# Layer 1's second mixer product as seven block products for two token tiles

## The chip, the cores and the metric

The kernel runs on one core of a Trainium2 chip. The metric is the device time of one execution in microseconds, the median of several runs. A core has TensorE (PE; its weight loads are shown as PEld), VectorE (DVE), ScalarE (ACT), GpSimd (POOL) and SyncE (SP), which here issues the DMAs. Each engine works through its own instructions in the order in which they are written, and waits where an operand is not there yet.

## The reference

Two layers, each of an attention and a token mixer, with the residual added after both. All is float32. The part that the change touches is the second matrix product of the mixer (`w2`), in the second layer:

```python
h = _layernorm(x, axis=-1)                      # (B, S, D)
u = jnp.einsum("bsd,sf->bdf", h, w1) + b1       # (B, D, F)
u = _gelu(u)
y = jnp.einsum("bdf,fs->bds", u, w2) + b2       # (B, D, S)
return y.transpose(0, 2, 1)                     # (B, S, D)
```

S = 2048 tokens, D = 512 channels, F = 1792. The output of the mixer, transposed, is w2^T u + b2, a matrix of 2048 x 512 with inner size 1792, added to x.

## The kernel before, in words

x is kept in SBUF as 16 token tiles of 128 x 512. Matrix products are done in a reduced float32 form (fp32r). To keep the precision, both operands are split in two: the first half is the value rounded to fp32r (a cast, mostly on ACT), the second half is what the rounding left (a subtraction, on DVE or POOL). A product is then three matmuls: first x first, first x second, second x first.

The order of all work is written out by hand (manual schedule), so the text's order is each engine's order. Layer by layer, `att.run` computes the attention and, between its parts, the first mixer product; `mix.rest` ends both. In `rest`, the last two pairs of token tiles are multiplied: first eight products of six matmuls, then twenty more (L1205), of which every second or so ends a tile f of 128 rows of u. When tile f is complete, `finish` adds it from PSUM on DVE (L1213). The local function `following` is called after each of the twenty products. It splits the w1 weights three products ahead (cast on ACT, L1190; subtraction on POOL, L1192) and loads those seven ahead; then it takes one waiting tile, in two calls of three: `gelu` (ACT: activation L1424, cast L1425), and one call later `gelu_rest` (DVE, L1429). What is left over is done after the last product.

For the second product, `load2` loads w2 in halves of a token tile's weights, 128 partitions x 7 tiles x 128 columns (448 KB), and `split2` splits such a half (ACT L1446, DVE L1447). `second(s)` does one token tile s: for each of the 14 tiles of F three matmuls of 512 columns (L1458) into one PSUM bank, 42 in all, then one DVE instruction adds the bias and x (L1464). In layer 1 the tile is then stored (L1608). The halves are split one and a half token tiles ahead, so a token tile costs ACT two casts and DVE two subtractions and one addition. The first two halves are loaded and split while the first product still runs. In layer 0 the same loop carries the projections of layer 1 between the token tiles; the change leaves layer 0 as it was.

PSUM holds three double banks (tag `sc`) and two single ones (`ac0`, `ac1`). At the end of layer 1 the tiles of the attention (`kst`, `qs`, `vaug`) hold nothing that is still needed, and neither do the mixer's accumulators `uacc` once their gelu is done.

Of the kernel before, what the change touches and what calls it, by code (L numbers as in the profile page):

```python
# [8 lines left out]
F32 = mybir.dt.float32  # L9
# [9 lines left out]
P = 128  # L19
# [12 lines left out]
LAG = 2  # L32
KEPT = 6
GOING = 8

# [16 lines left out]
PLAIN = (2, -2)  # L52
FIRST = (1, 2)
NP = 8
NMORE = 4
# [17 lines left out]
def kernel(  # L73
# [1004 lines left out]
    class Mixer:  # L1078
# [21 lines left out]
        def open(self):  # L1100
            n = self.l
            self.opened = True
            self.ap = pool(f"uacc{n}")
            self.wp = pool(f"w1p{n}")
            self.hp = pool(f"hp{n}")
            self.uacc = [self.ap.tile([P, D], F32, tag=f"ua{f}", name=f"ua{n}_{f}") for f in range(NF)]

# [172 lines left out]
        def rest(self, att):  # L1280
# [99 lines left out]
            def following():  # L1380
# [5 lines left out]
                if ahead is not None:  # L1386
                    begun.append(ahead)

            def rests():
# [26 lines left out]
        def open_u(self):  # L1416
            n = self.l
            self.up = pool(f"up{n}", side="right")
            self.w2p = pool(f"w2p{n}", side="right")
            self.u = [self.up.tile([P, 2, D], F32R, tag=f"u{f}", name=f"u{n}_{f}") for f in range(NF)]  # L1420

        def gelu(self, f):
            tmp = self.uacc[f]
            nc.scalar.activation(tmp, tmp, AF.Gelu_apprx_tanh, bias=b1c[:, f : f + 1])  # L1424
            nc.scalar.copy(self.u[f][:, 0, :], tmp)  # L1425

        def gelu_rest(self, f):
            tmp = self.uacc[f]
            nc.vector.tensor_tensor(self.u[f][:, 1, :], tmp, f32(self.u[f][:, 0, :]), op=ALU.subtract)  # L1429

# [39 lines left out]

        def close(self):
            self.w2p.release()
            self.up.release()
# [111 lines left out]
    for layer in range(2):  # L1585
        mix = Mixer(layer)
        att.run(mix, proj)
        mix.rest(att)
        more = layer == 0
        if more:  # L1590
            warm(AF.Exp)
            proj = Proj(layer + 1)
# [134 lines left out]
```

## Time and profile before

| | us |
|---|---|
| median of 3 runs | 2514.87 (2514.69 to 2514.93) |
| span of the profiled execution | 2509.2 |
| PE busy in it | 2492.8 (99%) |
| DVE, ACT, POOL busy | 1550.9, 2101.7, 148.2 |
| matmuls of line 1458, both layers: count, busy, mean | 1344, 307.4, 0.390 |

The profile is of one execution; its span leaves out some microseconds that the runs' time has. A row of the groups gives the line, the engine, what is written from what, the shapes, how often, the busy time in us and the mean of one in ns, and after a second bar the time for which the engine was idle ahead of these instructions and what ended that wait. Matmuls overlap one another, so their mean duration (0.390) is longer than the distance from one to the next. A row of a timeline gives start, duration, engine, line and operation, and how many instructions were merged.

### The profile page before, as it was taken

How to read it: one execution, taken by the hardware profiler on the slowest of the kernel's cores; microseconds unless marked ns; L12 is line 12 of the kernel's file. 1: busy time of each engine (PE TensorE's matmuls, PEld its weight loads, DVE VectorE, ACT ScalarE, POOL GpSimd, SP SyncE). 2: the span in 40 equal slices, each digit the busy share in tenths (PEclk: the TensorE clock that was granted, in tenths of full speed). 3: DMA queues.
4: the chain of work that ended last, by engine and by line, in shares of the span. 5: the costliest groups of instructions: out<-in, count | busy, mean ns of one | idle time of the engine just before them, and what ended most of it. 6: DMA issues, size and time to landing. Idle time of an engine off the chain costs nothing. (4 is left out here: it accounts for less than half of the span.)

```text
span 2509.2 us, 41946 instructions
## 1 busy us (share of the span) xinstructions
PE 2492.8 (99%) x16158; PEld 1240.5 (49%) x16158; DVE 1550.9 (62%) x2458; ACT 2101.7 (84%) x2344; POOL 148.2 (6%) x235
## 2 busy tenths in 40 slices
PE   8999999999999999999999999999999999999999
PEld 6444344444444444588863443444444444445887
DVE  6566566667766776564445664666677667765522
ACT  6999999999999999653349999999999999995511
POOL 5000000000000000141000000000000000002200
PEclk9999999999999999999999999999999999999999
DMA  3221201111111111144423211111111111102343
GB/s 117 75 66 41 65 28 40 31 42 31 39 31 39 31 40 32 41 112 149 126 61 118 58 48 48 31 39 33 39 31 39 32 43 33 40 26 67 106 125 96
DMA packets 168679, 143.56 MB, mean 57 GB/s; under 512 B 17650, under 2 KB 132368, under 8 KB 167952
## 3 DMA queue, kind: packets, MB, share of 16 engines
q1 hardware_dynamic: 168464, 140.72, 19.0%
q8 instruction: 132, 2.16, 0.4%
q14 instruction: 83, 0.68, 0.1%
HBM read 97.67 MB, written 26.22 MB: 49 GB/s over the span
## 5 line engine op out<-in xcount | busy, mean ns | idle before, releaser
L922 ACT ACTIVATE p<-sc 128x1024 f32<-128x1024 f32 x1444 | 1405.8, 1049 | 62.9 <-PE sc L912 62.2
L920 DVE COPY p<-sc 128x1024 f32<-128x1024 f32 x604 | 739.1, 1224 | 522.3 <-PE sc L912 436.4
L928 PE MATMUL acc<-p,vaug 128*32 128x512 f32 x8192 | 1000.1, 599 | 0.5 <-DVE q L531 0.5
L912 PE MATMUL sc<-qs,kst 51*128 51x512 f32 x4096 | 683.5, 432 | 6.8 <-SPq L630 2.7
L922 ACT ACTIVATE p<-p 128x1024 f32<-128x1024 f32 x604 | 655.9, 1086 | 14.1 <-DVE p L920 9.2
L912 PEld LDWEIGHTS sc<-qs,kst 51*128 51x128 f32 x4096 | 338.3, 184 | 559.5 <-ACT p L922 387.3
L928 PEld LDWEIGHTS acc<-p,vaug 128*32 128x32 f32 x8192 | 219.0, 109 | 489.3 <-issue 472.9
L1458 PE MATMUL py<-u,w 128*128 128x512 f32 x1344 | 307.4, 390 | 0.0
L1458 PEld LDWEIGHTS py<-u,w 128*128 128x128 f32 x1344 | 251.9, 188 | 52.3
L1446 ACT CAST w<-w2r 128x896 fp32r<-128x896 f32 x64 | 60.3, 945 | 184.6 <-PE py L1458 177.3
L1205 PE MATMUL pu<-hb,w 128*128 128x512 f32 x792 | 209.6, 406 | 0.0
L1205 PEld LDWEIGHTS pu<-hb,w 128*128 128x128 f32 x792 | 140.9, 188 | 57.7 <-issue 31.9
L1192 POOL TENSOR_TENSOR w<-w1r,w 128x256 fp32r<-128x256 f32 x86 | 70.0, 822 | 1581.5 <-ACT w L1190 1581.1
L1447 DVE TENSOR_TENSOR w<-w2r,w 128x896 fp32r<-128x896 f32 x64 | 72.0, 1124 | 111.4 <-ACT w L1446 111.2
L848 DVE RECIPROCAL o<-o 128x128 f32<-128x128 f32 x120 | 113.3, 944 | 9.4 <-DMA o<-ev 9.4
L889 PE MATMUL po<-wo,hl 128*128 128x512 f32 x360 | 100.4, 412 | 0.1
L830 DVE COPY ev<-acc 128x512 f32<-128x512 f32 x64 | 43.7, 682 | 62.1 <-PE acc L928 62.1
L418 PE MATMUL pq<-hT,wq 128*128 128x512 f32 x312 | 81.1, 404 | 0.0
L889 PEld LDWEIGHTS po<-wo,hl 128*128 128x128 f32 x360 | 62.6, 188 | 33.9 <-issue 16.0
L1205 PE MATMUL pu_l<-hb,w 128*128 128x512 f32 x336 | 77.1, 389 | 0.0
L1464 DVE SCALAR_TENSOR_TENSOR x<-py,b2c,x 128x512 f32<-128x512 f32 x32 | 24.0, 750 | 81.2 <-PE py L1458 81.2
L1190 ACT CAST w<-w1r 128x256 fp32r<-128x256 f32 x86 | 34.5, 406 | 47.1 <-PE pu_l L1205 14.3
(191 smaller groups left out, 1179.0 us busy)
## 6 DMA issues: line engine op xcount, KB each, us to landing
w1r<-in_B_w_dram SPq DMA_DIRECT2D x224, 128.0 KB
w2r<-in_B_w_dram SPq DMA_DIRECT2D x64, 448.0 KB
qs<-qd SPq DMA_DIRECT2D x384, 64.0 KB
qd<-q SPq DMA_DIRECT2D x64, 256.0 KB
o<-ev SPq DMA_DIRECT2D x128, 128.0 KB
x<-in_A_x_dram SPq DMA_DIRECT2D x16, 256.0 KB
hd<-hT SPq DMA_DIRECT2D x2, 2048.0 KB
out_dram<-x SPq DMA_DIRECT2D x16, 256.0 KB
```

Source lines behind the costliest of these rows:

```text
L418: yield nc.tensor.matmul(out, a, c, start=(k == 0), stop=(k == len(terms) - 1))
L848: nc.vector.reciprocal(o[:, 1, c], o[:, 1, c])
L889: nc.tensor.matmul(po, a, c, start=(k == 0), stop=(k == 3 * len(parts) - 1))
L912: nc.tensor.matmul(sc[:, j, :], kst[kt // 4][rows, kt % 4 * P : (kt % 4 + 1) * P], qs[i % NQ][rows, j0 // 2, :], start=True, stop=True,)
L920: nc.vector.tensor_copy(pt, sc)
L922: nc.scalar.activation(pt, sc, AF.Exp, scale=0.25)
L928: nc.tensor.matmul(self.acc[i][c : c + 32, :], vaug[:, kt].rearrange("p d k -> p (d k)"), pt[:, j, :], start=(kt == 0), stop=(kt == NKT - ...
L1192: eng.tensor_tensor(w[:, 1], raw, f32(w[:, 0]), op=ALU.subtract)
L1205: nc.tensor.matmul(pu, a, c, start=(start and k == 0), stop=(stop and k == 5))
L1446: nc.scalar.copy(w[:, 0], raw)
L1447: nc.vector.tensor_tensor(w[:, 1], raw, f32(w[:, 0]), op=ALU.subtract)
L1458: nc.tensor.matmul(py, a, d, start=(c == 0 and f == 0 and k == 0), stop=(c == 1 and f == NFH - 1 and k == 2),)
```

## The change: what it does

In layer 1 the second product is done for two token tiles at once by the Strassen-Winograd scheme. The weights of a pair of token tiles are four blocks A11, A12, A21, A22: the first digit is the token tile, the second says whether they belong to even or odd tiles of F. Each block is 128 x 7 x 128. u is cut likewise: B11 and B12 are the left and right 256 columns of the even tiles of F, B21 and B22 those of the odd ones. Instead of eight block products there are seven:

- outer sums of the weights, for each pair of token tiles: S1 = A21 + A22, S2 = S1 - A11, S3 = A11 - A21, S4 = A12 - S2. They are written over blocks no longer needed and are done by POOL (for the first pair of token tiles by DVE), 128 x 896 each;
- inner sums of u, once: T1 = B12 - B11, T2 = B22 - T1, T3 = B22 - B12, T4 = B21 - T2 (`inner_sums`, seven steps for each of the seven pairs k of tiles of F). The first difference of a pair k is on POOL for k < 4, else on DVE; the other two are on DVE. T1 takes the place of B12 in `u`; T2 and T3 are put in the freed accumulator of the pair, T4 in `kst` and `qs`; working tiles lie in the mixer's pool, or in `vaug` and a tile of the w2 pool. Each T is split into two halves (four casts on ACT, four subtractions on DVE, of 256 columns). `following` takes two of these steps a call; of those left, all but seven are done in `begin_pairs`, the last seven beside the first product;
- the gelu's cast and `gelu_rest` of even tiles are done for 256 columns, since B12 is not used itself.

`pairs` runs eight pairs of token tiles, each of seven products. A product is, for each of seven k, one matmul of 512 columns (the weights' first half times both halves of the 256 columns, side by side) and one of 256 columns (the weights' second half times the first half). One DVE instruction adds each half of the bank to x, so each use of a product is two instructions of 256 columns. In the first pair of token tiles the products go to six banks, in the other seven to three that are used again (X four times, where the second use goes on from the first without clearing it). The weights of product n + 3 are split when product n is written; blocks of the pair after next are loaded in the fifth product of a pair, four loads of 448 KB. `load_pair(0)` stands where the first two halves were loaded; the first split stands after the last gelu, and no weights are split within the first product any more. A token tile is stored after the sixth, its neighbour after the seventh product.

```diff
+PAIR = (
+    ("A11", "B11", "X", True, ("11b",)), ("A12", "B21", "Z", True, ("11",)),
+    ("S2", "T2", "X", False, ("12b",)), ("S1", "T1", "Y", True, ("22b",)),
+    ("S3", "T3", "X", False, ("22",)), ("S4", "B22", "Y", False, ("12",)),
+    ("A22", "T4", "X", False, ("21b",)),
+)
+FIRST_PAIR = (
+    ("A11", "B11", "X", True, ("11b",)), ("A12", "B21", "Z", True, ("11",)),
+    ("S1", "T1", "Y", True, ("12b", "22b")), ("S3", "T3", "W", True, ("21b", "22")),
+    ("S2", "T2", "X", False, ("12", "21", "22")), ("S4", "B22", "V", True, ("12",)),
+    ("A22", "T4", "U", True, ("21",)),
+)
...
             self.open_u()
             warm(AF.Gelu_apprx_tanh)
-            self.load2(0)
-            self.load2(1)
+            if n:
+                self.load_pair(0)
+            else:
+                self.load2(0)
+                self.load2(1)
             for k, pu in enumerate(going):
                 self.product(pu, start=False, stop=False)
                 self.following()
-                if k in (5, 7):
+                if not n and k in (5, 7):
                     self.split2((k - 5) // 2)
...
                 if ahead is not None:
                     begun.append(ahead)
+                for _ in range(2):
+                    if self.inner_steps:
+                        self.inner_steps.pop(0)()
...
             for g in late:
                 self.gelu(g)
                 self.gelu_rest(g)
+            if n:
+                self.begin_pairs()
+                return
             self.split2(2)
...
+            def first():
+                a = got["a"] = pair("ta")
+                eng = nc.gpsimd if k < 4 else nc.vector
+                eng.tensor_tensor(a, halves[:, :, 1], halves[:, 0], op=ALU.subtract)
+
+            def first_split():
+                t1 = self.u[2 * k][:, :, HD:]
+                split(t1, got["a"][:, 0])
+
+            def second():
+                b = got["b"] = pair("tb")
+                nc.vector.tensor_tensor(b[:, 0], halves[:, 1, 1], got["a"][:, 0], op=ALU.subtract)
+                nc.vector.tensor_tensor(b[:, 1], halves[:, 1, 0], b[:, 0], op=ALU.subtract)
+                self.t23[k] = self.ap.tile([P, 2, 2, HD], F32R, tag=f"ua{k}", name=f"t{n}_{k}")
+                split(self.t23[k][:, 1], got["a"][:, 1])
+                split(self.t23[k][:, 0], b[:, 0])
+                split(self.t4[k], b[:, 1])
...
+            return [first, first_split, second, first_low, third_low, second_low, fourth_low]
...
+        def split_pair(self, n):
+            q, j = divmod(n, len(PAIR))
+            if 2 * q >= NKT:
+                return
+            src = self.raw[q, (PAIR if q else FIRST_PAIR)[j][0]]
+            p, bufs = (self.w2q, 3) if n % 4 else (self.w2p, 1)
+            w = self.w2[n] = p.tile([P, 2, NFH, P], F32R, tag="w2", bufs=bufs, name=f"w2_{n}")
+            nc.scalar.copy(w[:, 0], src)
+            nc.vector.tensor_tensor(w[:, 1], src, f32(w[:, 0]), op=ALU.subtract)
+
+        def begin_pairs(self):
+            self.split_pair(0)
+            for name in ("S1", "S3"):
+                self.outer_sum(0, name, nc.vector)
+            while len(self.inner_steps) > 7:
+                self.inner_steps.pop(0)()
+            self.hp.release()
+            self.wp.release()
+            self.w2q = pool("w2q")
+            self.load_pair(1)
+            self.split_pair(1)
+            self.split_pair(2)
...
+            for j, (left, right, key, start, outs) in enumerate(PAIR if q else FIRST_PAIR):
+                n, py = len(PAIR) * q + j, banks[key]
+                self.split_pair(n + 3)
+                w = self.w2.pop(n)
+                for k in range(NFH):
+                    t = self.operand(right, k)
+                    nc.tensor.matmul(
+                        py.rearrange("p (k c) -> p k c", k=2), w[:, 0, k], t,
+                        start=start and k == 0, stop=False, skip_group_check=True,
+                    )
+                    nc.tensor.matmul(
+                        py[:, :HD], w[:, 1, k], t[:, 0], start=False, stop=(k == NFH - 1),
+                        skip_group_check=True,
+                    )
+                if q == 0:
+                    self.beside_first(j)
+                elif j == 2:
+                    self.outer_sum(q + 1, "S1")
+                    self.outer_sum(q + 1, "S3")
+                if j == 4:
+                    self.load_pair(q + 2)
+                    self.outer_sum(q + 1, "S2")
+                if j == 5:
+                    self.outer_sum(q + 1, "S4")
+                for out in outs:
+                    s, c = 2 * q + int(out[0]) - 1, slice((int(out[1]) - 1) * HD, int(out[1]) * HD)
+                    if out[2:]:
+                        nc.vector.scalar_tensor_tensor(
+                            x[s][:, c], py[:, :HD], b2c[:, s : s + 1], x[s][:, c], op0=ALU.add, op1=ALU.add
+                        )
+                    else:
+                        nc.vector.tensor_tensor(x[s][:, c], x[s][:, c], py[:, :HD], op=ALU.add)
+                    nc.vector.tensor_tensor(x[s][:, c], x[s][:, c], py[:, HD:], op=ALU.add)
+                if j > 4:
+                    s = 2 * q + j - 5
+                    nc.sync.dma_start(xout[:, s, :], x[s])
+
+        def beside_first(self, j):
+            if j == 0:
+                self.outer_sum(0, "S2", nc.vector)
+                for step in self.inner_steps:
+                    step()
+                self.outer_sum(0, "S4", nc.vector)
+            if j == 2:
+                self.outer_sum(1, "S1")
+                self.outer_sum(1, "S3")
```

More of the change, by code (lines that the diff above doesn't have):

```diff
@@ new lines, in pair_pool, with load_pair @@
+        def pair_pool(self, q):
+            return self.w2q if q % 2 else self.w2p
+        def load_pair(self, q):
+            if 2 * q >= NKT:
+                return
+            for j, name in enumerate(RAWS):
+                s, c = 2 * q + j // 2, j % 2
+                src = w2_d[:, s * P : (s + 1) * P].rearrange("(t c p) s -> c p t s", p=P, c=2)[c]
+                raw = self.pair_pool(q).tile([P, NFH, P], F32, tag=f"r{name}", name=f"r{name}_{q}")
+                nc.sync.dma_start(raw, src)
+                self.raw[q, name] = raw
@@ L1589 @@
         more = layer == 0
+        if not more:
+            mix.pairs()
+            mix.close()
+            break
         if more:
```

81 lines of the change are left out of this document (76 added, 5 removed).

## The prediction

> **What bounds the kernel now.** I read the page first, then groups by line, then the queues around the end of layer 1's first mixer product, then its steady second product.
>
> ```profile
> span 2509.2 us, 41946 instructions
> PE   8999999999999999999999999999999999999999
> PE 42%; DVE 1%; ACT 0%; issue 0%; DMA 0%; DVEq 0%; ACTq 0%
> PE acc L928 16%; PE sc L912 11%; PE py L1458 6%; PE pu L1205 4%; PE po L889 2%; PE pu_l L1205 2%; PE pq L418 1%; PE pu_m L1205 0%; DVE p L920 0%; ACT p L922 0%; PE pu_b L1205 0%; PE pu_a L1205 0%; PE pu_e L1205 0%; PE po_l L889 0%; DVE stb L1118 0%
> L1458 PE MATMUL py<-u,w 128*128 128x512 f32 x1344 | 307.4, 390 | 0.0
> L1458 PEld LDWEIGHTS py<-u,w 128*128 128x128 f32 x1344 | 251.9, 188 | 52.3
> ```
>
> TensorE is never idle ahead of line 1458 (0.0) and carries the chain. Half of its 1344 matmuls, 672, are layer 1's. The profiled execution spans 2509.2 us and the median of the runs is 2514.87, so 5.7 us lie outside the span; the sum below is a difference, laid on the median. The pace is in DVE's evacuations, one for each token tile:
>
> ```profile
> 2400.54 0.75 DVE L1464 SCALAR_TENSOR_TENSOR x<-py,b2c,x 128x512 f32<-128x512 f32 x1 [2.69 <-PE py L1458]
> 2410.06 0.75 DVE L1464 SCALAR_TENSOR_TENSOR x<-py,b2c,x 128x512 f32<-128x512 f32 x1 [2.69 <-PE py L1458]
> ...
> 2505.25 0.75 DVE L1464 SCALAR_TENSOR_TENSOR x<-py,b2c,x 128x512 f32<-128x512 f32 x1 [8.77 <-PE py L1458]
> ```
>
> 9.52 us for 42 matmuls is 226.7 ns each; 16 token tiles are 152.3 us. Beside it DVE, ACT and POOL are nearly idle. The stage ahead is another matter:
>
> ```profile
> 2333.00:2353.00 20.00, 20.00 (x90) 16.56 (x89) 12.66 (x20) 17.63 (x34) 10.56 (x12) 1.00 0.22 61
> 2330.93 21.92 PE L1205 MATMUL pu_l<-hb,w 128*128 128x512 f32 x96
> 2352.69 9.50 PE L1458 MATMUL py<-u,w 128*128 128x512 f32 x41
> 2353.61 0.72 ACT L1424 ACTIVATE ua<-ua,b1c 128x512 f32<-128x512 f32 x1
> 2354.36 0.62 ACT L1425 CAST u<-ua 128x512 fp32r<-128x512 f32 x1
> 2354.89 0.94 ACT L1446 CAST w<-w2r 128x896 fp32r<-128x896 f32 x1
> ```
>
> The columns of the first are busy time of PE, loads, DVE, ACT, POOL. In the last 20 us of the first product ACT is busy for 17.63 and DVE for 12.66. PE goes straight from one product to the other, while the last gelu ends two microseconds later: it is wanted only at the end of the first token tile, whose weights were split long before.
>
> **The change on TensorE.** For two token tiles there were 84 matmuls of 512 columns; now there are 7 products x 7 tiles, each with one of 512 and one of 256: 49 pairs, 392 over the eight pairs of token tiles. No row has 256 columns. Two rows are near:
>
> ```profile
> 10.30 2.84 PE L137 MATMUL pt<-ident 128*128 128x128 f32 x24
> L137 PEld LDWEIGHTS pt<-ident x24: 192/192/192, 10.2 to 12.8; 128*128 128x128 f32 x24
> L137 PE MATMUL pt<-ident x24: 275/275/275, 10.3 to 12.9; 128*128 128x128 f32 x24
> ```
>
> 24 matmuls, each with its own load recorded at 192 ns, follow one another every (2840 - 275) / 23 = 111.5 ns. So a load that is shown with 188 ns need not hold the array for longer than 111.5. The low end is half of 226.7, 113.4; the high end is a matmul held until its load's recorded end, 188. I take 118, close to the half, since part of the 226.7 may be fixed. A pair is 344.7 ns and the stage 392 x 344.7 = 135.1 us: **17.2 us less** (19.0 by the low end; 10.3 more than before by the high one). A product lasts 2.41 us.
>
> The Trainium skill (TensorE: Matmul & The Clock Gate, Back-to-back issue gap) gives columns / 2.4 + 2.5 ns. By it a pair would be 325 ns and the stage 127 us, 25 us less; at 512 columns it says 215.8 where the row above has 226.7, so the row decides.
>
> **What the other engines get.** The rows for their prices:
>
> ```profile
> L1447 DVE TENSOR_TENSOR w<-w2r,w 128x896 fp32r<-128x896 f32 x64 | 72.0, 1124 | 111.4 <-ACT w L1446 111.2
> L1192 DVE TENSOR_TENSOR w<-w1r,w 128x256 fp32r<-128x256 f32 x138 | 58.7, 425 | 4.8
> L1190 ACT CAST w<-w1r 128x256 fp32r<-128x256 f32 x86 | 34.5, 406 | 47.1 <-PE pu_l L1205 14.3 <-PE pu_b L1205 7.4 <-DMA w1r<-in_B_w_dram 6.8
> L1192 POOL TENSOR_TENSOR w<-w1r,w 128x256 fp32r<-128x256 f32 x86 | 70.0, 822 | 1581.5 <-ACT w L1190 1581.1
> L327 POOL TENSOR_TENSOR wq<-wqr,wq 128x512 fp32r<-128x512 f32 x2 | 2.5, 1284 | 0.0
> 2336.57 1.28 DVE L1213 TENSOR_TENSOR ua<-ua,pu_l 128x512 f32<-128x512 f32 x2 [0.69 <-PE pu_l L1205]
> 2309.89 0.74 POOL L1192 TENSOR_TENSOR w<-w1r,w 128x256 fp32r<-128x256 f32 x1 [0.60 <-ACT w L1190]
> 2309.95 1.23 DVE L1342 TENSOR_TENSOR hb<-ht,hb 128x512 fp32r<-128x512 f32 x1
> ```
>
> Two DVE instructions of 0.69 us end after 1.28, so each overlaps the next by about 0.08: I count 0.345 for 256 columns, 0.61 for 512, 1.02 for 896, and 0.31 for ACT's cast. An evacuation of 256 columns is put at 0.4: 0.75 less 256 x 1.04 ns (the step from 0.69 at 512 to 1.09 at 896), less the overlap. From 256 to 512 POOL goes from 0.74 to 1.28, 2.1 ns a column, so 896 columns cost about 2.15. The last two rows: a DVE subtraction of two SBUF tiles, 0.69 elsewhere, takes 1.23 beside POOL's, that is until 0.55 after POOL's end at 2310.63. It waits its turn; what the two take turns at is called the port below.
>
> I then laid the queues out in the order of the code.
>
> *A, the tail of the first product.* In its last fifteen products of six matmuls (1.36 us each), 30 of the 49 steps of the inner sums are pulled in. ACT gets 17 casts, 5.3 us, less 1.3 for shorter gelu casts: 21.6 us for 20. Worse is the order. Four of the differences are on POOL, 1.28 us each, behind a w1 subtraction of 0.74 that waits for an ACT cast; ACT's cast of the result stands ahead of the next w1 cast. ACT so waits 1.0 to 2.4 us four times, some 6 in all, and DVE's new subtractions and POOL's stop one another. That is 7.6 us over; w1 casts run three products ahead (4.08, less 0.41 for the cast and 0.74 for POOL: 2.9 of lead), so PE stalls about 5. SP adds four w2 loads at once where there were two, then two:
>
> ```profile
> w2r<-in_B_w_dram SPq DMA_DIRECT2D x64, 448.0 KB
> 2315.00:2320.00 5.00, 5.00 (x23) 4.14 (x23) 4.62 (x15) 1.92 (x6) 2.79 (x4) 1.00 0.84 228
> 2321.33 0.78 ACT L1190 CAST w<-w1r 128x256 fp32r<-128x256 f32 x2 [2.00 <-DMA w1r<-in_B_w_dram]
> ```
>
> With two, the next w1 cast already came 1.0 us behind its beat; 0.92 MB more is 3 to 4 us at these rates, against the lead of 2.9: about 1 us on PE. A with DVE and POOL's mutual waits: **6.5** (2 if ACT's waits fill its idle time, 9 if not).
>
> *B, from the last matmul to the first product.* The weights' split now stands behind the last gelu. The floor is on the rows above: addition 0.69, gelu and cast 1.37, split 0.94, subtraction 1.09: 4.1 us, all idle on PE. With ACT's backlog (three casts, two gelus, a wait for DVE, gelu 12) it is 9.3 if all of it is left: I take **8**.
>
> *C, the first pairs.* Before the second product's weights, DVE has two sums of 896 (2.04), twelve steps' worth of inner sums (twelve instructions of 256 columns and one of 512: 4.75) and the subtraction, 1.02: 7.8 us, while PE has 2.41. So at least **5.4** more. Further stalls follow: the last tile's inner sums (2.7) and S2 (1.02) stand in DVE's queue between, and POOL's S1 and S3 for the next pair, 2 x 2.15, want the same port as soon as the loads land; then evacuations of up to six instructions of 0.4 keep DVE behind until the second pair. In the layout the second product waits 6.8 in all (5.4, and ACT's casts between DVE's steps), the third 0.7, or 4.5 if S1 and S3 get in between the last tile's differences, the fifth 1.1 for its bank, the eighth to tenth 2.3, or 4.8 with the port: 10.9 without the port, 17 with it. I take **14**.
>
> *D, steady state.* DVE has 7 x 1.02 + 14 x 0.4 = 12.7 us of a pair's 16.9, ACT 7 x 0.85 = 6, POOL 4 x 2.15 = 8.6. POOL and DVE's subtractions together hold the port for 15.7, and POOL's sums come in pairs, so an evacuation can stand behind a subtraction that stands behind POOL, while PE waits for its bank. Up to 0.9 a pair for six pairs, 5.4; or 0. I take **3.5**. The loads (1.84 MB in 17 us) move what they did before, a pair ahead, and are hidden, as are SP's stores until the last; the last evacuation is two instructions of 0.4 for one of 0.75: 0.1.
>
> The Trainium skill (SBUF — State Buffer, Who interferes with whom) states it as an exclusive lock between GpSimd and DVE instructions with two SBUF inputs, none for those with one. By it C and D are near their upper ends and the sum is 5 us more; without it they are 10.9 and 0, and the sum is 7 us less. The two rows above agree with it.
>
> Sum: -17.2 + 6.5 + 8 + 14 + 3.5 + 0.1 = +14.9 on 2514.87: **2530 us**.
>
> **Rivals.**
>
> *The start is cheap.* If inner sums fit ACT's and DVE's idle time (DVE has 7.3 us idle in those 20, POOL 9.4) only the floors are left: -19.0 + 2 + 4.1 + 5.4 = -7.5, **2507 us**, faster. It decides once A to D stay under 17.2 less 5. Against it: the queues are in order, and each step crosses three engines.
>
> *Loss and gain cancel.* ACT meets POOL's results without waiting (A 2, B 6) and C is 10.9: -17.2 + 18.9 + 0.1 = +1.8, **2517 us**.
>
> *POOL and DVE do not collide.* A 5, B 8.4, C 10.9, D 0: +7, **2522 us**.
>
> *Loads hold the 256-column matmuls*, at 188 ns or as long as 512 columns take, so that the seven products save nothing: the stage is 27.4 us longer than counted, D vanishes: 2530 + 27.4 - 3.5 = **2554 us**. The 111.5 ns row speaks against it.
>
> **How the numbers follow.** Forecast (2524 to 2540) 0.47, start cheap 0.21, cancel 0.13, no collision 0.13, loads 0.06. About 0.2% (5 us) is what a measurement here can tell from no change. Faster is the first rival, 0.21; same the second, 0.13; slower the rest, 0.66. Range 2507 to 2541: the first rival's time to the upper ends of all four, -17.2 + 9 + 9.3 + 17 + 5.4 = +23.5, and a little for a slower 256; outside lie the loads and what beats the floors. The forecast alone spans 2524 to 2540.
>
> **What would show it.** PE's pitch of the new matmuls: 345 ns a pair in an undisturbed product. PE idle ahead of the first product 4 to 9 us, released by ACT or DVE, and ahead of the second at least 5, released by DVE: if either is missing, B or C is wrong. PE waiting for w1 from POOL or ACT after 2335 us shows A. DVE subtractions of 896 columns with means well over 1.1 us, ending a fixed time after POOL's, show the port. A stage under 150 us from the first product's last matmul to the last evacuation (2352.85 to 2506.00, 153.2, before) would make the whole wrong.

## The result, and the profile after

The changed kernel takes 2572.73 us (median of 4, 2571.23 to 2573.88) beside 2514.85 of the kernel before: 1.0234 times as long, 95% interval 1.0219 to 1.0248. It is slower, as forecast, but by 57.9 us instead of 15, and the time lies above the range. One of the twelve executions of the last kernel below (e15) took 4724.9 us; its ratio is of the other eleven.

The page of the changed kernel, its TensorE row in 40 slices, and its chain by engine:

```profile
span 2572.1 us, 42521 instructions
PE   9999999999999999999999999999999999997688
...
DVE 4%; PE 3%; ACT 1%; issue 0%; DMA 0%; POOL 0%; ACTq 0%
```

Before, the chain was TensorE's and its row never fell below 9 after the first slice. Now the last four slices are 7, 6, 8, 8, and VectorE heads the chain. Stretches of the end of layer 1 (busy time of PE, PEld, DVE, ACT, POOL, then the granted clock), first of the changed kernel, then the first product's tail before:

```profile
2318.30:2364.30 46.00, 40.62 (x169) 30.52 (x167) 30.54 (x61) 25.48 (x61) 25.19 (x30) 1.00 0.40 106
2364.00:2372.00 8.00, 0.65 (x3) 0.19 (x1) 5.95 (x13) 6.61 (x13) 0.00 (x0) 0.83 0.61 172
2372.00:2376.90 4.90, 4.32 (x14) 3.24 (x14) 4.55 (x8) 0.82 (x4) 0.00 (x0) 0.59 0.00 0
2376.90:2394.00 17.10, 0.16 (x2) 0.00 (x0) 16.30 (x25) 6.59 (x14) 5.75 (x2) 0.57 0.10 27
2414.00:2438.00 24.00, 19.56 (x101) 16.48 (x100) 18.67 (x22) 6.89 (x8) 11.10 (x6) 0.93 0.38 110
2438.00:2459.00 21.00, 17.34 (x97) 14.70 (x97) 17.19 (x22) 6.25 (x7) 9.62 (x4) 1.00 0.37 107
```

```profile
2314.60:2352.50 37.90, 37.90 (x169) 31.38 (x168) 25.20 (x45) 26.95 (x54) 21.83 (x26) 1.00 0.46 129
```

The same 169 matmuls of the tail take 46.0 us instead of 37.9. Then come 8 us with TensorE idle, one product of 14 matmuls at little over half the granted clock (0.59), and 17 us idle in which VectorE works 16.3. The last two rows of the changed kernel are its second and third pairs of token tiles: TensorE stands idle for 4.4 us of 24 and 3.7 of 21. What TensorE waited for after 2364 us (total, times, longest):

```profile
PE py L1595 <- DVE x L1621: 35.1, 8, 17.1
PE py L1595 <- ACT w L1551: 15.0, 8, 7.6
PE pyw L1595 <- DVE x L1621: 1.9, 1, 1.9
```

And single matmuls of TensorE, then the VectorE instructions ahead of the two waits (start, duration):

```profile
2376.78 0.28 PE L1599 MATMUL py<-u,w 128*128 128x256 f32 x1
2394.19 0.77 PE L1595 MATMUL py<-u,w 128*128 128x512 f32 x1 [17.13 <-DVE x L1621]
...
2427.62 0.40 PE L1595 MATMUL pyy<-u,w 128*128 128x512 f32 x1
2437.46 0.40 PE L1595 MATMUL py<-u,w 128*128 128x512 f32 x1
2439.80 0.28 PE L1599 MATMUL py<-u,w 128*128 128x256 f32 x1
2442.68 0.47 PE L1595 MATMUL py<-u,w 128*128 128x512 f32 x1 [2.60 <-DVE x L1621]
```

```profile
2381.25 1.09 DVE L1552 TENSOR_TENSOR w<-rA,w 128x896 fp32r<-128x896 f32 x1 [0.35 <-ACT w L1551]
2382.26 2.96 DVE L1552 TENSOR_TENSOR w<-rS,w 128x896 fp32r<-128x896 f32 x1
...
2393.11 0.48 DVE L1616 SCALAR_TENSOR_TENSOR x<-py,b2c,x 128x256 f32<-128x256 f32 x1
2393.62 0.42 DVE L1621 TENSOR_TENSOR x<-x,py 128x256 f32<-128x256 f32 x1
...
2439.53 2.15 DVE L1552 TENSOR_TENSOR w<-rS,w 128x896 fp32r<-128x896 f32 x1
2441.61 0.47 DVE L1616 SCALAR_TENSOR_TENSOR x<-py,b2c,x 128x256 f32<-128x256 f32 x1
2442.11 0.42 DVE L1621 TENSOR_TENSOR x<-x,py 128x256 f32<-128x256 f32 x1
...
2445.87 0.42 DVE L1621 TENSOR_TENSOR x<-x,py 128x256 f32<-128x256 f32 x1
```

The second product's weights were ready at 2382.3 (the 1.09 us subtraction). TensorE did not begin until 0.15 us after the first product's evacuation had ended, at 2394.04. The same 0.15 us stands behind the evacuation that ends at 2442.53, in a later pair; there the evacuation is late behind a weight subtraction of 2.15 us. The second product writes Z, not X; Z and X are the two halves of the tile `both`. That is what the first experiment takes apart. From 2427.62 to 2437.46 four products without a wait take 9.84 us, 351 ns for each pair of matmuls.

The second row of the waits is two things: one wait of 7.6 us ahead of the first product, and seven of 1.06 ahead of the third product of a pair. For these the profile names ScalarE's cast, which ended last. The evacuation of Z (2445.87 us in the rows above) ended 0.12 us earlier, at 2446.29, and the product began at 2446.44, again 0.15 us behind the evacuation; in the first experiment these waits are released by evacuations too.

The profile of the kernel before is of an execution that is quicker than its median. In the changed kernel the profiled execution took 2573.88 us and spans 2572.1, so 1.8 us lie outside the span, not the 5.7 of the prediction; by that the one profiled before took about 2511 us. So the two spans differ by 62.9 us and the medians by 57.9.

### The profile page after: what moved, and what is told of

It reads as the page before. It is cut to its first block, busy times and chain, and to the rows that moved or that the text cites. A ratio compares the mean times of both kernels' runs of the same rounds, so it can differ in the third digit from the quotient of the medians.

```text
span 2572.1 us, 42521 instructions
## 1 busy us (share of the span) xinstructions
PE 2497.7 (97%) x16270; PEld 1241.6 (48%) x16270; DVE 1667.4 (65%) x2635; ACT 2132.5 (83%) x2396; POOL 221.5 (9%) x267
## 5 line engine op out<-in xcount | busy, mean ns | idle before, releaser
L1663 PE MATMUL py<-u,w 128*128 128x512 f32 x672 | 154.8, 390 | 0.0
L1663 PEld LDWEIGHTS py<-u,w 128*128 128x128 f32 x672 | 125.7, 188 | 26.1
L1551 ACT CAST w<-rA 128x896 fp32r<-128x896 f32 x48 | 45.2, 941 | 108.2 <-PE py L1599 82.1
L1651 ACT CAST w<-w2r 128x896 fp32r<-128x896 f32 x32 | 30.0, 943 | 76.9 <-PE py L1663 69.3
L1595 PE MATMUL py<-u,w 128*128 128x512 f32 x112 | 48.3, 459 | 42.7 <-DVE x L1621 35.1
L844 DVE COPY ev<-acc 128x512 f32<-128x512 f32 x64 | 43.7, 682 | 62.8 <-PE acc L942 62.8
L1552 DVE TENSOR_TENSOR w<-rA,w 128x896 fp32r<-128x896 f32 x48 | 75.1, 1565 | 2.7 <-ACT w L1551 0.4
```

Of the source, the lines that this page charges most:

```text
L1551: nc.scalar.copy(w[:, 0], src)
L1552: nc.vector.tensor_tensor(w[:, 1], src, f32(w[:, 0]), op=ALU.subtract)
L1595: nc.tensor.matmul(py.rearrange("p (k c) -> p k c", k=2), w[:, 0, k], t, start=start and k == 0, stop=False, skip_group_check=True,)
L1663: nc.tensor.matmul(py, a, d, start=(c == 0 and f == 0 and k == 0), stop=(c == 1 and f == NFH - 1 and k == 2),)
```

## The experiments

The runs of one execution are read by their traces, by the length of a stretch: the attention ahead of it arrives up to 6.4 us apart (2287.1 to 2293.5 us at the first matmul into `pu_a`) in kernels that share it. On the chips of the experiments the kernel before takes 2510.6 to 2511.8 us, beside 2514.85 where the changed kernel ran, so a difference of 4 us between two times can be the chip. The stretch from the last first-product matmul to the end of the span is 207.9 us in the changed kernel.

**X, Z and Y in tiles of their own (e1).**

```diff
-            both = bank2(f"py_{q}")
-            banks = {"X": both[:, 0], "Z": both[:, 1]}
+            second = bank2(f"pyz_{q}")
+            banks = {"X": bank2(f"pyx_{q}")[:, 0], "Z": second[:, 0]}
...
-                more = bank2("pyw")
-                banks.update(Y=more[:, 0], W=more[:, 1], V=bank(0, "pyv"), U=bank(1, "pyu"))
+                banks.update(Y=bank2("pyw")[:, 0], W=second[:, 1], V=bank(0, "pyv"), U=bank(1, "pyu"))
```

> The blocks' accumulators X and Z, which are two halves of one tile of two banks in the changed kernel, lie in two tiles here (likewise the first pair's Y; W shares a tile with Z). Theory, the wait is by tile: a product into Z waits for the evacuation of X, and the next one into X for that of Z, though their banks are apart. Then the second product of the first pair begins when its weights are ready, 5 to 7 us after the first ends instead of 17.1; W's wait of 1.9 goes; in the other seven pairs the second product's 2.6 to 2.9 us and the third's 1.06 us fall under 1 us together; the products that began cold after those waits run warm. Time 2520 to 2540 us (2572.7 less 10 to 12 at the first pair, less 7 times 2.7 to 3.8, less 2 to 9 of cold clock). Rival, the evacuations come late because VectorE is late with them (GpSimd's sums and VectorE's splits hold one another up), and the tiles don't matter: the waits only move to another product of the pair, and the time stays over 2560 us.

2535.78 us (4 executions), 1.0096 times the kernel before (1.0079 to 1.0113). TensorE's waits:

```profile
PE pyx L1594 <- ACT w L1551: 7.6, 1, 7.6
PE pyz L1594 <- DVE x L1620: 4.3, 1, 4.3
PE pyz L1594 <- ACT w L1551: 3.5, 1, 3.5
PE pyx L1594 <- DVE x L1620: 2.7, 6, 1.0
PE pyz L1598 <- DVE w L1552: 2.5, 1, 2.5
```

The wait is by tile. The second product now starts when its weights come (3.5 us, and 2.5 more inside it), the second products of the other pairs do not wait at all, and the third ones' 7 times 1.06 us are 2.7 us in all. The stretch is 172.1 us, 35.8 less, by moving nothing but accumulators. W, which I left in one tile with Z, waits 4.3 us here for Z's evacuation; in the changed kernel it shares a tile with Y and waits 1.9. Half clock is left in the first pair only (its seven products take 9.4 us more than the 2.345 that an undisturbed one has from its first matmul to its last; 3.0 of the 9.4 are waits inside them, the rest half clock). In the traces these are waits for semaphores (in the changed kernel an EVENT_SEMAPHORE of line 1595 on the queue of TensorE's loads, at 2394.1), so they are waits that the program sets. The new tiles lie in other pairs of banks as well; whether it counts by tile or by the pair of banks that a tile covers, e1 does not tell.

**The first evacuation ahead of the sums beside it (e2).**

```diff
                 if q == 0:
-                    self.beside_first(j)
+                    pass
...
+                if q == 0:
+                    self.beside_first(j)
                 if j > 4:
```

> Only the order on VectorE in the first pair changes: the evacuation of its first product (0.8 us) stands ahead of the second outer sum, the last inner sum's seven steps and the fourth outer sum instead of behind them. Theory, the wait is by tile: the second product of the first pair begins 5 to 8 us after the first ends instead of 17.1, the later pairs keep their waits (2.6 to 2.9 and 1.06 us): 2560 to 2565 us. Rival, the second product waits for its operands (the inner sums, the split weights) and not for the evacuation: its wait stays over 14 us, and the time within 2 us of 2572.7.

2568.2 us, and 203.7 for the stretch, 4.2 less. The wait falls from 17.1 to 11.9 us: shorter, not the 5 to 8 expected. The rows of VectorE above say why. Two weight subtractions of 2.95 us beside GpSimd's sums stand ahead of the evacuation in either order. What the wait is for shows here as well, the evacuation having moved. Its end on VectorE and the second product:

```profile
2386.89 0.42 DVE L1621 TENSOR_TENSOR x<-x,py 128x256 f32<-128x256 f32 x1
...
2387.46 0.77 PE L1595 MATMUL py<-u,w 128*128 128x512 f32 x1 [11.88 <-DVE x L1621]
```

The product has moved with it and begins 0.15 us behind its end, again.

**Without GpSimd's outer sums in pairs one to seven (e3).**

```diff
             raw = {k: self.raw[q, k] for k in RAWS}
+            if q:
+                self.raw[q, name] = raw[{"S1": "A21", "S2": "A11", "S3": "A21", "S4": "A12"}[name]]
+                return
```

> GpSimd's 28 outer sums of pairs one to seven are left out (the products S1 to S4 of those pairs take unsummed weight blocks of the same size, so the output is not the reference's). Tests how much of the steady state is GpSimd and VectorE holding one another up. Theory, the wait is by tile, and GpSimd only lengthens it: VectorE's split of 128x896 goes from 2.95 to about 1.57 us where GpSimd's sum ran beside it; the second product's wait in each pair falls from 2.6-2.9 to 1.0-1.5 us and the third's 1.06 stays: 2560 to 2566 us. Rival, the collisions are the cause: both waits go, and the time falls to 2548 us or less.

2552.7 us. The weight subtractions of the changed kernel in all eight pairs, then those of this one in pairs one to seven:

```profile
L1552 DVE TENSOR_TENSOR w<-rA,w 128x896 fp32r<-128x896 f32 x48 | 75.1, 1565 | 2.7 <-ACT w L1551 0.4
```

```profile
L1555 DVE TENSOR_TENSOR w<-rA,w 128x896 fp32r<-128x896 f32 x45 | 49.2, 1093 | 2.7
```

TensorE's wait for the evacuations in this kernel, the answer to the 35.1 us above:

```profile
PE py L1598 <- DVE x L1624: 20.8, 8, 12.9
```

The mean falls from 1565 to 1093 ns. The seven second products' waits fall from 2.6 to 1.1 us each (20.8 less 12.9, over 7), and the third's 1.06 stays. So GpSimd makes the evacuation late, and the shared tile makes TensorE wait for it. The time fell by 20.0 us, further than expected, and the stretch by 19.6: 14.3 are this row's (4.2 of them in the first pair, whose subtractions met the next pair's sums), 4.6 are half clock (5.8 us of it instead of 10.4). The granted clock is 1.00 from 2392.6 to 2549 us, so waits of 1.1 and 1.06 us a pair did not bring it down.

**The first pair's loads staggered (e4).**

```diff
-                self.load_pair(0)
+                self.load_pair(0, (0, 1))
...
-                if not n and k in (5, 7):
-                    self.split2((k - 5) // 2)
+                if k in (5, 7):
+                    if n:
+                        self.load_pair(0, (2 + (k - 5) // 2,))
+                    else:
+                        self.split2((k - 5) // 2)
```

> Only the four loads of the first pair's weight blocks move: two are issued at the start of the first product's tail, as in the kernel before, and two after its products 5 and 7. Tests the part of A that I did not price: in the changed kernel the four loads of 448 KB stand ahead of a first-product weight on SyncE's queue, ScalarE waits 5.8 us for that weight, and TensorE about 2 to 3 us. Theory: that stall goes, and the first product's last matmul comes 2 to 3 us earlier than in the changed kernel (about 2361.5 on its axis), with nothing else changed: 2569 to 2571 us. Rival: the tail is held by ScalarE, VectorE and GpSimd anyway and takes the gain back: within 1 us of 2572.7.

2579.0 us, more than the changed kernel. The stall was there to be removed. In the changed kernel ScalarE has this row:

```profile
2328.74 1.54 ACT L1206 CAST w<-w1r 128x256 fp32r<-128x256 f32 x4 [5.76 <-DMA w1r<-in_B_w_dram]
```

With the loads staggered, TensorE goes from the first matmul into `pu_a` to the last one in 37.0 us, as in the kernel before (36.9), instead of 38.9. From the same first matmul to the last one of the first product it has 69.6 us (62.8 before the change, 71.0 after), so 0.6 of the 2.0 is lost again behind it. What made the kernel slower is elsewhere, in the second and third products of the later pairs: 3.2 and 4.0 us from first matmul to last where the changed kernel has 3.9 at most and mostly 2.4. TensorE in one of these, of this kernel, and three stretches around it:

```profile
2437.94 0.47 PE L1600 MATMUL py<-u,w 128*128 128x512 f32 x1 [2.60 <-DVE x L1626]
...
2439.45 0.63 PE L1600 MATMUL py<-u,w 128*128 128x512 f32 x1
...
2445.98 0.50 PE L1600 MATMUL py<-t,w 128*128 128x512 f32 x1
```

```profile
2436.00:2439.40 3.40, 1.46 (x8) 1.30 (x9) 3.37 (x4) 0.32 (x1) 2.83 (x1) 1.00 0.68 187
2439.40:2446.20 6.80, 5.74 (x19) 4.60 (x18) 2.38 (x4) 0.94 (x1) 0.00 (x0) 0.50 0.12 33
2446.20:2449.60 3.40, 3.40 (x20) 2.93 (x20) 2.12 (x4) 1.07 (x2) 0.00 (x0) 1.00 0.73 204
```

In the middle of a product, 1.4 us after the wait, the granted clock (third number from the right) drops to 0.50 for 6.8 us and comes back. That belongs to no engine's queue; the next two runs are on it.

**Filling TensorE's waits (e10, e13).** Small matmuls of a constant into an unused bank, added to the staggered kernel; the second run has half as many.

```diff
+                if q and j < 2:
+                    spare = bank(q + 1, f"warm_{q}_{j}")
+                    heat((22, 8)[j], spare)          # second run: (11, 4)
```

> The kernel with the loads staggered (2577.2 us of span, its second and third products of each pair at half the clock) with small matmuls of a constant into a spare bank where TensorE waits in pairs one to seven: 22 before the second product, 8 before the third. They add no data anyone reads. Theory: the half-speed products are the granted clock falling while TensorE waits, not contention for its operands: the second and third products of a pair take 2.3 to 2.45 us each instead of 3.2 and 4.0, the waits themselves stay about as long, and the time falls by 10 to 17 us, to 2562 to 2569. Rival: they are slow because VectorE, GpSimd and the weight loads share the memory then: durations stay, and the time is 2577 us or more.

> The staggered kernel with half as many filling matmuls (11 before the second product and 4 before the third, 2.4 and 0.9 us at the pitch measured with 22 and 8), so that they are shorter than the waits. Theory: second and third products stay at 2.4 us, the waits of 2.6 and 1.06 us still end with the evacuation, and the time is 10 to 17 us under the staggered kernel's 2579.0: 2562 to 2569. Rival: a wait left over of a few tenths is enough for the clock to fall again: 2575 us or more.

2583.2 and 2565.1 us. In both, the second and third products take 2.38 to 2.44 us in every pair from the second on. A stretch of the second run that holds one of each, with the fillers:

```profile
2433.40:2442.40 9.00, 8.68 (x60) 7.75 (x59) 6.63 (x7) 1.88 (x2) 3.70 (x2) 1.00 0.31 84
```

The clock stays at 1.00 while VectorE and GpSimd work as before, so the half-speed products were the clock and not contention. The first run was too generous: each filler shows as two matmuls of 112 ns, so 22 and 8 of them last 4.8 and 1.7 us against waits of 2.6 and 1.06. The second fits, and 14 us fall away, as forecast (15.0 by the stretch, 203.7 for 218.7).

**The first weights split earlier (e5); the first differences on VectorE (e6).**

```diff
+                if n and k == 7:
+                    self.split_pair(0)
...
-            self.split_pair(0)
             for name in ("S1", "S3"):
```

> The split of the first product's weights is issued eight products earlier, so ScalarE and VectorE do it before the first product's tail. Theory (the prediction's): the 7.6 us in which TensorE stands between its last first-product matmul and the first block product are ScalarE's queue and then the split itself; with the split done early the wait is for the last GELU and its cast, 4 to 6 us, and the time falls by 1 to 4 us if nothing at the first pair's second product takes it back; that product is released by the evacuation of X, behind VectorE's sums, and these start no earlier, so the time falls by 0 to 2 us: 2570.5 to 2573. Rival: the wait was for the split alone: it falls under 2 us and the time by 5 or more.

```diff
-                eng = nc.gpsimd if k < 4 else nc.vector
+                eng = nc.vector
```

> The four first differences of the inner sums that GpSimd makes in the first product's tail (1.3 to 1.5 us each, between two weight splits that TensorE waits for) are made by VectorE (0.7 us). Theory: GpSimd's queue was what delayed the first product's weights, and VectorE has room: the tail ends 1 to 4 us earlier, 2568.5 to 2571.5 us. Rival: VectorE is as loaded, and the tail ends at the same time or later: 2572 us or more.

The first takes 2575.8 us. Rows of TensorE in it:

```profile
2362.28 0.40 PE L1596 MATMUL py<-u,w 128*128 128x512 f32 x1
2368.39 0.79 PE L1596 MATMUL py<-u,w 128*128 128x512 f32 x1 [3.21 <-DVE u L1468]
2390.73 0.77 PE L1596 MATMUL py<-u,w 128*128 128x512 f32 x1 [21.34 <-DVE x L1622]
```

The first product starts at once and waits 3.6 us inside for the last gelu (0.4 and 3.2), and the second waits 21.3 us instead of 17.1. From the last first-product matmul to the second block product it is 28.7 us against 29.9: the gain is handed on to the next wait, as the theory had it. The rest, to 3 us more than the changed kernel, is half clock in later pairs (11.3 us against 5.5).

The second takes 2584.0 us. Its tail has 70.5 us against 71.0: VectorE is as loaded as GpSimd, and which of them makes the differences does not matter. Here too the difference in time is clock (17.1 us in later pairs).

**Four plain tiles first (e8, e9, e11).** If the start is what costs, the inner sums should be made beside products that do not need them. These kernels give the first four token tiles the plain product of the kernel before, keep T1 aside until its place in `u` is free, and make six pairs of Strassen products. The core, against the changed kernel:

```diff
-            for q in range(NKT // 2):
+            for s in range(2 * PLAINS):          # PLAINS = 2
+                self.second(s)
+                self.after(s)
+                nc.sync.dma_start(xout[:, s, :], x[s])
+            for q in range(PLAINS, NKT // 2):
                 self.pair(q)
```

> The first product's tail is again the one of the kernel before (no inner sums in it, two weight loads), the first four token tiles take the plain second product of the kernel before, and the inner sums are made beside those 38 us; the other six pairs are Strassen products with X, Z and Y in tiles of their own. Theory (the loss was the start and the tile waits; the saving of about 2.0 us a pair is real): six pairs save 12.2 us, the third product's wait of 0.3 to 1 us a pair gives 2 to 4 back, and nothing is lost at the start: 7 to 11 us under the kernel before, 2500 to 2508 us on this chip's axis. Rival, VectorE doesn't get the inner sums done in 38 us beside GpSimd's sums, or the first block products wait for T1 to T4: a stall of 5 to 15 us at the sixth pair's start and a time from the kernel before's to 5 us over it.

> As the kernel with four plain tiles first, with T3 formed from the right difference and the work beside ordered by its due time: the inner sums stand ahead of the splits on VectorE, GpSimd makes its differences three ahead, the first block weights are split one half product after another, and in each pair VectorE evacuates a product before it splits weights for the third next. Theory (what was left over the saving were VectorE's order and the start of the sixth pair, 8.5 us there and 3 us of waits of the third product): TensorE runs without a wait over 0.3 us from the first plain product to the end; six pairs save 6 times 1.97 us: 2498.5 to 2502 us where the kernel before takes 2510.9. Rival: VectorE and GpSimd together are full in the steady state, and a wait of 0.3 to 1.2 us a pair stays whatever the order: 2504 to 2509 us.

> As the tuned kernel with four plain tiles, with another order beside the plain tiles only: inner sums begin while the last first-product tiles are split, two a half product, a tile's evacuation one half product later, each block's weights loaded and split as soon as their buffers come free, and the seventh pair's loads after the first block product, so that GpSimd's next sums don't meet VectorE's splits of T1. Theory: the sixth-from-last pair then begins without a wait (8.6 us of waits and half-speed products there go), the 0.46 us a pair of the fifth product stay: 2502 to 2505 us beside 2511 of the kernel before. Rival: the waits move to the next pair and the time stays within 2 us of the kernel before.

The first of these forms T3 from B22 - B21 where it should be B22 - B12, so its output is not the reference's; the instructions are as many and as large. It takes 2510.9 us, ratio 0.9996 (0.9987 to 1.0006). The tuned one takes 2511.5, ratio 0.9996 (0.9987 to 1.0005), the third 2513.8, ratio 1.0014 (1.0004 to 1.0023). All three missed: the loss of 57.9 us is gone, and not one shows the saving. Each has 5 to 9 us of waits where plain tiles end and Strassen pairs begin, at another place each time.

**Three matmuls of 256 columns (e12).** The terms of a tile go into the same 256 columns, and one evacuation reads them instead of two.

```diff
-                    nc.tensor.matmul(
-                        py.rearrange("p (k c) -> p k c", k=2), w[:, 0, k], t,
...
+                    for i, (a, d) in enumerate(split_terms(w[:, 0, k], w[:, 1, k], t[:, 0], t[:, 1])):
+                        nc.tensor.matmul(
+                            py[:, :HD], a, d, start=start and k == 0 and i == 0,
...
-                    nc.vector.tensor_tensor(x[s][:, c], x[s][:, c], py[:, HD:], op=ALU.add)
```

> As e11_start, but a block product's three terms are three matmuls of 256 columns into the same 256 columns of the bank instead of one of 512 and one of 256, so that VectorE evacuates 256 columns once instead of twice (14 operations of 0.42 us a pair become 8). Measures what a weight load costs when every matmul has 256 columns. Theory by the pitches here (256 columns after 512: 115 to 120 ns): 3 times 116 is 348 ns a triple, the same as now, and VectorE's 3 us a pair less take away the fifth product's wait: 1 to 3 us faster than e11_start. Rival, a load of 188 ns cannot hide behind a matmul of 116: 564 ns a triple, 9 us a pair more: 2555 us or more.

2511.4 us, 2.4 less than the kernel it is built on. Three matmuls take 358 ns (2.505 us a product), not 564, and not quite 348. Its waits are 2.9 us at the third plain tile, 1.1 and 0.6 in the first pair, 2.3 in the next. The first had a plain reason: ScalarE cast the inner sums before the weights, VectorE sat 2 us each half product waiting for that cast, and a plain tile's evacuation came late.

**The queues beside the plain tiles put in order (e14, and e15 with 512 and 256 columns).** The cast of a weight block goes first on ScalarE, and VectorE does an inner sum while it waits for it.

```diff
             nc.scalar.copy(w[:, 0], raw)
+            between()
             nc.vector.tensor_tensor(w[:, 1], raw, f32(w[:, 0]), op=ALU.subtract)
...
+            def sums():
+                if h < 7:
+                    self.inner_lows(h)
+                self.inner_sums(h + 1)
...
+                self.split2(h + 3, sums)
```

> As e12_cols256 (four plain tiles, then six pairs with three matmuls of 256 columns), with one more order beside the plain tiles: ScalarE casts a weight block before the inner sums' casts and VectorE does an inner sum between that cast and its own half of the split, so that neither waits for the other each half product; the seventh pair's loads and its first two GpSimd sums come before the sixth pair begins. Theory (what e11 and e12 lost were 2.9 us at the third plain tile, 1.1 and 0.6 in the first Strassen pair, 2.3 in the next, all of them VectorE and ScalarE waiting on one another, and 2 us of half clock behind them): all four waits go, six pairs of 17.5 us stand for six of 19.05: 2502 to 2506 us, beside 2511 of the kernel before. Rival: a wait of that size comes back elsewhere at the change from plain to Strassen: within 2 us of the kernel before.

> The same with the block product's matmuls of 512 and 256 columns and two evacuations. Measures, beside e14_ordered, what the halved evacuation is worth against the pitch (119 ns per 256 columns measured when all have 256, 115 and 231 when they alternate). Theory: 17.07 us a pair of matmuls and 0.46 us of wait a pair, equal to e14's 17.5: within 2 us of e14_ordered. Rival: the fuller VectorE brings the start's waits back, and it is 3 to 8 us slower than e14_ordered.

2502.48 us with 256 columns, ratio 0.9962 (0.9949 to 0.9975): faster than both kernels. With 512 and 256 columns 2508.3, ratio 0.9990 (0.9981 to 0.9999). TensorE in the faster one as the second product begins; its only wait after 2353 us; two stretches of steady pairs:

```profile
2352.80 38.62 PE L1551 MATMUL py<-u,w 128*128 128x512 f32 x168
2391.27 2.67 PE L1618 MATMUL pyx<-u,w 128*128 128x256 f32 x21
2393.77 2.68 PE L1618 MATMUL pyz<-u,w 128*128 128x256 f32 x21
```

```profile
PE pyy L1618 <- DVE x L1625: 0.2, 1, 0.2
```

```profile
2409.00:2427.00 18.00, 18.00 (x153) 18.00 (x152) 16.02 (x15) 7.16 (x8) 10.24 (x5) 1.00 0.56 161
2427.00:2445.00 18.00, 18.00 (x153) 18.00 (x152) 15.52 (x16) 7.09 (x8) 10.54 (x5) 1.00 0.46 134
```

Six pairs of 17.5 us (18.0 the first) stand for six of 19.04, some 8.6 us less. The medians differ by 9.3, and the stretch by 8.5 (148.2 us, 156.7 in the kernel before). Between e12 and e14 the work is the same and its order differs, and TensorE's 6.8 us of waits become 0.2: in these kernels the loss where the pairs begin was the order of the queues. With 512 columns TensorE still waits 5.3 us (4.0 for evacuations, 1.3 for T1), as the rival had it.

## Why the prediction was right and wrong

From the last first-product matmul to the end of the span the kernel before has 156.7 us and the changed one 207.9. The difference, 51.1, is made of: matmuls -14.6 (392 pairs of 351.4 ns against 152.3 us), then the gaps between products beyond that pitch, 7.9 ahead of the first, 19.4 in the first pair and 28.0 in the other seven, and what the products last longer than an undisturbed one, 10.4, nearly all of it half clock. Ahead of it the tail is 8.1 longer and started 3.7 later, within the scatter of the attention. Against the sum of the prediction that is 24.5 us more in D, 10.4 of clock that it did not have, 5.4 more in C, 2.6 less saved, and 1.6 more in A.

*The pitch* was nearly right: 351 ns a pair where I had 344.7, 2.6 us short over the stage. The rival that loads hold the 256 columns is refuted by e12 as well.

*A* was right: 8.1 for 6.5, inside 2 to 9. The loads are 2.0 of it, where I had 1. ScalarE waits 5.5 us for GpSimd's four differences, where I had some 6, but that counts for little: with the same differences on VectorE the tail is only 0.5 us shorter (e6).

*B* was right: 7.9 for 8. That it was ScalarE's backlog ahead of the split is shown by e5, which leaves only the last gelu's 3.6.

*C* was wrong in its main term. "The second product waits 6.8 in all" is 17.1: the product waited for the evacuation of X, which I had laid behind S2, the last tile's inner sums and S4 without asking who waits for it. With tiles apart (e1) it is 6.0, 3.5 ahead and 2.5 inside. The sign named for C, at least 5 us released by VectorE, came out in the changed kernel all the same, by this other mechanism, and so proved nothing. Of the smaller ones, the third product waits 0 (0.7 or 4.5 forecast), the fourth 1.9, the ninth and tenth 4.4 (2.3 or 4.8).

*D* was the step that failed: 28.0 us where the sum has 3.5. It says that "an evacuation can stand behind a subtraction that stands behind POOL, while PE waits for its bank. Up to 0.9 a pair for six pairs, 5.4; or 0". The mechanism, GpSimd holding up VectorE, was there (e3 takes 1.5 us a pair away). Beside VectorE's subtractions of 2.96 and 2.95 us in the rows of the result, GpSimd has

```profile
2381.32 2.95 POOL L1536 TENSOR_TENSOR rS<-rA,rA 128x896 f32<-128x896 f32 x1 [17.93 <-DMA rA<-in_B_w_dram]
2384.36 2.80 POOL L1541 TENSOR_TENSOR rA<-rA,rA 128x896 f32<-128x896 f32 x1
```

and each subtraction ends some 0.95 us after the sum beside it, the sign that the prediction named for the port. But I counted the wait by bank, with a product's time of slack between writing X and writing it again. It is by tile: a product into Z waits for X, the next into X waits for Z, with no slack, 2.6 and 1.06 us a pair. e1 leaves 2.7 us for all seven later pairs, near what the sum had (3.5).

*Not in the sum at all* was the clock. The waits make TensorE idle enough to lose half its clock: some 10 us here, and 11 to 17 us in the later pairs alone of e4, e5 and e6.

So the sum comes nearest to e1, the kernel whose two banks are two tiles: 1.0096 times the kernel before, where the sum said 1.006. Even there 24.4 us were lost and not 15, part of it to the clock. The rival "the start is cheap" was wrong of this kernel. e14 keeps the saving of six pairs, with the sums off the start and beside four plain tiles; that eight pairs could start without loss is not shown.

## What to carry to other kernels

Ask of each write whether it shares a tile, not only a bank, with what is still to be read: two accumulators that alternate want two tiles. Work moved beside a busy engine is free only when each in-order queue has it behind what the busy engine wants next, so order a cast, the work that can fill its latency, and then its consumer. A wait on TensorE can cost more than its length: 2.6 and 1.06 us a pair took some 2.5 us more in clock in e4, and 1.1 and 1.06 took none in e3. So look at the granted clock behind each wait before pricing it.

## What the hardware showed that was not expected

The clock falls by a fixed beat. In the staggered kernel (e4) it falls at 2439.38, 2463.27, 2487.16, 2511.05 and 2534.95 us, 23.9 us apart, each time for 6.8 us. In the changed kernel it falls at 2420.4, 2464.8 and 2509.2 us, 44.4 us apart, each time for 3.4. The Trainium skill (TensorE: Matmul & The Clock Gate, What's actually happening) says that activity is judged in free-running windows of 3413 ns. The traces agree: 23.9 is seven such windows and 44.4 thirteen, and half clocks of 3.4 and 6.8 us are one and two. By this a pair that waits 3.7 us can lock to the beat and lose clock in every pair (e4, e6: 23.9 us a pair), or in every second one (the changed kernel: 21.4 and 22.9 us in turn). In the pair between two falls of the changed kernel the same wait (2440.1 to 2442.7 us) is cut by the edge of such a window at 2440.9, six windows behind the fall at 2420.4: that leaves 0.8 us idle to the one and 1.8 to the other, and the clock stays at 1.00. That this is why edits that shorten a wait came out slower is my reading of e4 to e6; the runs with fillers show that idle time brings the fall about.

The Trainium skill (TensorE: Matmul & The Clock Gate, Why this matters for your kernels) advises against idle gaps of over 3 us. Here gaps of 2.6 us were enough: in e4, in the 3.4 us ahead of the fall at 2439.4, TensorE was idle for 1.94.

When every matmul has 256 columns, weight loads are busy all the time (18.00 of 18.00 us above) and the pitch is 119 ns; alternating with 512 columns, 256 take 115 to 120 and the pair 351. The Trainium skill (TensorE: Matmul & The Clock Gate, LDWEIGHTS) has columns / 1.2 ns for a load, from which I estimate 107 ns for 128 columns; the 119 measured decides.
